# Expert products of 512 columns, on two column groups and into one bank, in a fused attention, mixture and gated-unit kernel

## The chip, the cores and the metric

The kernel runs on one core of a Trainium2 chip. The metric is the device time of one execution in microseconds (us): 532.63 us, the median of three runs (532.57 to 532.8). The trace comes from one more execution, the profiled one.

## What is computed

Three stages follow one another, all in float32.

```python
p_packed = sm_attn(p, k, v)                 # 8 batches, 8 heads, 32 packed queries
x = sm_attn(q, p_packed, p_packed)          # 4608 tokens of 512
logits = x @ phi                            # 32 slots, 4 for each of 8 experts
d = softmax(logits, over tokens)
slot_input = d.T @ x                        # (8, 4, 512)
for e in range(8):
    h = maximum(slot_input[e] @ w1[e], 0)   # w1[e]: 512 x 1024
    slot_out[e] = h @ w2[e]                 # w2[e]: 1024 x 512
x = softmax(logits, over slots) @ slot_out
out = (sigmoid(x @ w_gate) * (x @ w_val)) @ w_out     # d_ff = 1536
```

`sm_attn` is softmax attention. The change lies in the loop over the experts and around it.

## The kernel before

**Stages.** The attention (to about 118 us) works batch by batch after an order written out by hand. The experts follow (to about 161 us), then the gated unit (to the end), which works through units of 768 tokens by 128 columns of `d_ff`, each in three parts. Each part has six products of 512 columns into `o_ps` and one `gate_value` for the unit ahead. Nothing of the gated unit can start before all experts are done: it multiplies by `gst`, which `g_product` makes from the transposed outputs `sot` of all slots.

**Weights.** The weights of the experts lie as 256 blocks of 128 x 256 numbers (128 KB): for each expert 16 blocks of `w1`, then 16 of `w2`. The first 15 blocks come in one transfer into `extra`, the others in 27 transfers `wt` of nine blocks, the last one of seven (blocks 249 to 255). `load` (line 155) gives each transfer a slot of a pool. A slot that is used again has to be read to the end first, and since SyncE issues transfers in the order of the program, one that waits for its slot holds up those behind it. The script's step `loads` issues, after the weights 14 to 25, the three 512 KB pieces of chunk 0 of the gated unit (`wg`, `wv`, `wo`), then the last weights, then the pieces of chunk 1 and of the later chunks. The `wv` of chunk 1 takes the slot that the transfer of blocks 240 to 248 used.

**An expert.** `up(e)` (line 742) has 16 products, for k in 0 to 3 and j in 0 to 3, of 256 columns each. The stationary operand is 32 wide, and j chooses one of four column groups of TensorE, so that the result lies as 4 x 32 partitions by 256 columns. A float32 product is two instructions in the trace. `rectify(e)` (line 756) is ScalarE's ReLU into `hs`. `flip(e)` (line 761) transposes `hs` in two pieces, and VectorE copies the expert's columns into `htz`, which is zero elsewhere. `down(e)` (line 772) has 16 products of 256 columns, for k in 0 to 7 and two halves n, with column group `k % 4`; half n goes into the bank `so_ps[n]`, in which all experts accumulate. In `down(7)`, before block 249, `warm(LAST_WARM)` (lines 663, 777) puts eight filler products of 128 columns.

**Order.** `script` (line 826) gives the order of the steps on every engine; an engine keeps its program order. `up(e)` runs two lines ahead of `down(e - 2)`. Between them lie `cst_turn` (line 713, TensorE transposes the token weights into a bank of `q_g`, of which there are two) and `cst_stack` (line 724, ScalarE and VectorE copy a batch out of it in turns, GpSimd copies on). `turn2` needs the bank that the stacks of batches 0 to 3 read. `decode_open` (line 811) decodes chunk 0: for each of three pieces ScalarE's `high`, VectorE's `shift`, ScalarE's `scale`, VectorE's `add`, and then ScalarE's `w_high` into `wo_parts`. It stands behind `flip7` and before `down7`.

**Tail.** ScalarE and VectorE copy the two halves of `so_ps` into `sos` (lines 869, 870), a short filler follows, then `sot_product` for both halves, copies, `g_product` (16 products on two column groups, 64 wide), another filler, `g_one`, and the gated unit begins. Chunk 1's decode (`a`, `b`, `o`) lies between these on ScalarE and VectorE; `b` is the `wv` of chunk 1.

**Pace.** In the gated unit the generator `readying` (line 931) prepares the weights of later units in small steps, one of which is `g_product`. `pace(part)` (line 1072) says how many steps a part takes, so that each is done when it is due.

Of the kernel before, what the change touches and what calls it, by code (L numbers as in the profile page):

```python
# [35 lines left out]
EPS = 1e-9  # L36
GOES = [(0, 0, 2), (1, 0, 3), (2, 0, 4), (0, 2, 6), (1, 3, 8), (2, 4, NF), (0, 6, NF), (1, 8, NF)]
WARM = 2
LAST_WARM = 8

EXTRA = 15
FIRST_WARM = 4
# [7 lines left out]
def kernel(  # L50
# [101 lines left out]
        places[0] += 1  # L152
        return head if places[0] % (HEADS + RING) in (1, 2) else ring

    def load(dst, key, src, name, last=False):
        i = turn[0] - 3 * B
        turn[0] += 1
        if i < SLOTS:
            r = i % SLOTS
            if r < TWIN:  # L160
                if r == 0:
                    twin.append(keep.tile([128, TWIN * SLOT], F32, name="twin", tag="cst"))
                t = twin[-1][:, SLOT * r : SLOT * r + SLOT]
            else:
                pool = ring if r < TWIN + RING else home if r < TWIN + RING + HOME else more
        elif last:
            pool = next_pool()
        else:

            r = i - SLOTS - HEADS - 3  # L170
            pool = once if r < -1 else spare if r < 0 else ring if r < RING else home if r < RING + HOME else more
            if r < -3:
                pool = head
        if i >= SLOTS or r >= TWIN:
            t = pool.tile([128, WB * EXTRA if pool is spare else SLOT], F32, name=name, tag="w")
        if src.dtype == F32:
            dst[key] = t[:, 0 : src.shape[-1]]
            nc.sync.dma_start(out=dst[key], in_=src)
        else:
# [12 lines left out]
    for i, (x, b) in enumerate("k0 k1 v0 q0 k2 v1 q1 k3 v2 q2 k4 v3 q3 v4 k5 q4 k6 k7 v5 q5 q7 v6 v7 q6".split()):  # L192
        b = int(b)
        for r in (slice(0, 1), slice(1, B))[i : i + 1]:
            nc.sync.dma_start(out=praw[:, r], in_=pd[:, r])
            (nc.gpsimd if i else nc.vector).tensor_scalar_mul(out=praw[:, r], in0=praw[:, r], scalar1=0.125)
        dst, src = dict(k=(kt, kd), v=(vt, vd), q=(qt, qd))[x]
        load(dst, b, src[b], x + "t")
        if i == 1:
            for r in range(2):  # L200
                rows = slice(64 * r, 64 * r + 64)
                nc.sync.dma_start(out=phi[rows, :, r, :], in_=phid[rows])

    def load_weights(a, z):
        for i in range(a, z):
            load(wt, i, wd[:, WB * (EXTRA + WS * i) : WB * min(EXTRA + WS * i + WS, NW)], "wt")

    nc.sync.dma_start(out=extra, in_=wd[:, 0 : WB * EXTRA])
    load_weights(0, SLOTS)
# [412 lines left out]
    q_a = pmid.enter_context(tc.tile_pool(name="q_a", bufs=4, space=PSUM))  # L622
# [36 lines left out]
    def qa():  # L659
        return q_a.tile([128, 512], F32, name="qa", tag="qa")  # L660


    def warm(n=WARM):
        ps = qa()
        for _ in range(n):
            pe.matmul(ps[:, 0:128], lhsT=i16, rhs=i16, start=True, stop=True)

    ps = qa()
    pe.transpose(ps[:, 0:128], prun, ident)
# [59 lines left out]
            for q in (0, 1):  # L729
                pool.tensor_copy(out=s[32 * q + 64 : 32 * q + 96], in_=s[32 * q : 32 * q + 32].bitcast(F32))  # L730

    so_ps = [q_so.tile([128, 512], F32, name=f"so_ps{n}") for n in range(2)]

    def block(e, i):
        i += 32 * e - EXTRA
        if i < 0:
            return extra[:, WB * (i + EXTRA) : WB * (i + EXTRA + 1)]
        return wt[i // WS][:, WB * (i % WS) : WB * (i % WS) + WB]

    hidden = {}  # L740

    def up(e):
        ps = qa()
        for k in range(4):
            for j in range(4):
                pe.matmul(
                    ps[32 * j : 32 * j + 32, 0:WB],
                    lhsT=xt[:, PERM[k], :],
                    rhs=block(e, 4 * k + j),
                    start=k == 0,  # L750
                    stop=k == 3,
                    tile_position=(0, 32 * j),
                )
        hidden[e] = ps

    def rectify(e):
        hs = e2p.tile([128, 256], F32, name="hs")
        act.activation(hs, hidden[e][:, 0:256], AF.Relu, scale=zr)
        hidden[e] = hs

    def flip(e):
        hs, ps = hidden[e], qa()
        for i in range(2):
            pe.transpose(ps[:, 128 * i : 128 * i + 128], hs[:, 128 * i : 128 * i + 128], ident)
        htz = hidden[e] = e2p.tile([128, 4, 2, NS], F32, name="htz")
        dve.memset(htz, 0.0)
        dve.tensor_copy(
            out=htz[:, :, :, 4 * e : 4 * e + 4],
            in_=ps[:, 0:256].rearrange("p (i j s) -> p j i s", i=2, j=4)[:, :, :, 4 * e : 4 * e + 4],
        )  # L770

    def down(e):
        for k in range(8):
            for n in range(2):
                j = k % 4
                if 32 * e + 16 + 2 * k + n == EXTRA + WS * (NWT - 1):
                    warm(LAST_WARM)
                pe.matmul(
                    so_ps[n][32 * j : 32 * j + 32, 0:WB],
                    lhsT=hidden[e][:, k // 2, k % 2, :],  # L780
                    rhs=block(e, 16 + 2 * k + n),
                    start=e == 0 and k < 4,
                    stop=e == E - 1 and k >= 4,
                    tile_position=(0, 32 * j),
                )


    def w_parts(x, f0, n):
# [33 lines left out]
    def split_first():  # L822
# [2 lines left out]

    script = """
        up0 slots_sub sums loads cst_open rectify0 slots_exp
        up1 rectify1 flip0 slots_sum
        up2 rectify2 down0 flip1
        up3 rectify3 down1 flip2 turn0  # L830
        up4 rectify4 down2 flip3 turn1 stack0 stack1
        up5 rectify5 stack2 down3 flip4 stack3
        turn2 up6 rectify6 stack4 down4 flip5 stack5
        down5 flip6 stack6
        up7 rectify7 down6 stack7 flip7 decode_open down7
    """
    steps = dict(up=up, rectify=rectify, flip=flip, down=down, turn=cst_turn, stack=cst_stack)
    alone = dict(
# [27 lines left out]
            )  # L866
        return sot[n].rearrange("p i r s -> p (i r s)"), ps[:, 0:128]

    act.copy(out=sos[0], in_=so_ps[0][:, 0:WB])
    dve.tensor_copy(out=sos[1], in_=so_ps[1][:, 0:WB])  # L870
    w_low(0, 1, w0[2].w)
    a.high()
    a.shift()
    warm()
    s0, s1 = sot_product(0), sot_product(1)
    act.copy(out=s0[0], in_=s0[1])
    dve.tensor_copy(out=s1[0], in_=s1[1])
# [28 lines left out]
    warm()  # L906
    g_one(0, first)
    b.scale()
    a.add()
# [193 lines left out]
    for n, (t, f, a, z) in enumerate(units):  # L1103
# [3 lines left out]
        for part in range(NH):  # L1107
# [95 lines left out]
```

## Time and profile before

| | us |
|---|---|
| median of three runs | 532.63 |
| profiled execution, its own time | 532.35 |
| its span in the trace | 530.6 |
| TensorE busy in the span | 507.0 (96%) |
| VectorE, ScalarE busy | 330.2 (62%), 288.5 (54%) |
| granted TensorE clock, mean | 0.994 of full speed |

The span begins and ends with the program's own instructions; the execution's own time has 1.75 us around it. Times in the rows further down are us from the start of the span. PE is TensorE's products and PEld its weight loads, DVE is VectorE, ACT ScalarE, POOL GpSimd, SP SyncE, which issues transfers. Behind an instruction stands, in brackets, how long its engine had been idle before it and what ended that. The ends of products are modelled, their starts recorded.

### The profile page before, as it was taken

Reading aid. Unit: us, or ns where it says so; the run is one execution under the profiler, and the core shown is the slowest. Engines: PE = TensorE matmul, PEld = TensorE weight load, DVE = VectorE, ACT = ScalarE, POOL = GpSimd, SP = SyncE. Lnnn points to the kernel's source line nnn. Section 1 sums busy time; section 2 is a strip of 40 time slices with the busy share of each in tenths; the row PEclk is TensorE's granted clock in tenths of the full one; section 3 lists DMA queues with packets and bytes.
Section 4 is the critical chain, followed back from the end, with each engine's and each line's share of the span. In section 5 each row is a group of like instructions: output and inputs, shape, how many; then the busy total and the mean of one; then the engine's idle time right before and its main releaser. Section 6 shows DMA issues by size and latency. Waiting matters only on the chain.

```text
span 530.6 us, 10825 instructions
## 1 busy us (share of the span) xinstructions
PE 507.0 (96%) x4217; PEld 394.4 (74%) x4217; DVE 330.2 (62%) x797; ACT 288.5 (54%) x749; POOL 58.4 (11%) x137
## 2 busy tenths in 40 slices
PE   8869989999888999999999999999999999999996
PEld 4536667665546787878888888888888888888885
DVE  2457869864357888889796654674445544454443
ACT  2656777633347878969585444444445444454443
POOL 4021413311540000210101000000000000000000
PEclk9988999999999999999999999999999999999999
DMA  8999999999999163360100120330001200030003
GB/s 326 420 419 418 418 420 419 417 419 418 420 387 397 73 233 119 125 240 13 67 0 1 42 79 1 119 118 3 1 1 41 79 2 0 1 119 2 1 1 119
DMA packets 18642, 91.45 MB, mean 172 GB/s; under 512 B 2336, under 2 KB 2720, under 8 KB 12064
## 3 DMA queue, kind: packets, MB, share of 16 engines
q1 hardware_dynamic: 18592, 90.77, 42.6%
q8 instruction: 33, 0.54, 0.4%
q14 instruction: 17, 0.14, 0.1%
HBM read 81.33 MB, written 9.44 MB: 171 GB/s over the span
## 4 chain that ended last, share of the span: by engine, by line
PE 82%; DMA 10%; DVE 3%; ACT 2%; issue 2%; SPq 0%; DVEq 0%; ACTq 0%
PE o_ps L81 54%; PE qg L81 11%; DMA wt<-in_w_dram 5%; DMA vt<-in_v_dram 3%; PE qa L81 2%; PE pq L81 2%; PE sq L81 2%; PE tq L81 2%; PE tps L81 1%; PE ta L81 1%; PE tp L81 1%; PE lp L81 1%; PE sp L81 1%; DMA kt<-in_k_dram 1%; PE lt L81 1%
## 5 line engine op out<-in xcount | busy, mean ns | idle before, releaser
L81 PE MATMUL o_ps<-wo_parts,gh 128*128 128x512 f32 x864 | 271.5, 395 | 0.5 <-ACT gh L81 0.5
L81 DVE TENSOR_TENSOR gv<-gv,qg 128x256 f32<-128x256 f32 x215 | 89.7, 418 | 126.3 <-ACT gv L81 125.4
L81 PE MATMUL o_ps<-wo_parts,gl 128*128 128x512 f32 x432 | 168.2, 389 | 0.0
L81 ACT ACTIVATE gv<-qg 128x256 f32<-128x256 f32 x215 | 82.5, 385 | 153.3 <-PE qg L81 153.1
L81 PEld LDWEIGHTS o_ps<-wo_parts,gh 128*128 128x128 f32 x864 | 147.8, 189 | 20.4 <-ACT gh L81 0.9
L81 PEld LDWEIGHTS o_ps<-wo_parts,gl 128*128 128x128 f32 x432 | 81.2, 188 | 18.8 <-DVE gl L81 0.3
L81 PEld LDWEIGHTS qg<-cst,gst 128*128 128x128 f32 x430 | 79.4, 188 | 19.5 <-DVE gv L81 1.3
L81 DVE TENSOR_TENSOR gl<-gv,gh 128x256 fp32r<-128x256 f32 (+1 forms) x217 | 90.2, 416 | 0.8 <-ACT gh L81 0.2
L81 ACT CAST gh<-gv 128x256 fp32r<-128x256 f32 (+1 forms) x217 | 86.6, 400 | 4.1 <-DVE gv L81 3.7
L81 PE MATMUL qg<-cst,gst 128*128 128x256 f32 x430 | 86.0, 283 | 0.1
L81 ACT ACTIVATE wgv<-wgv 128x512 f32<-128x512 f32 (+3 forms) x32 | 29.2, 927 | 1.4 <-DMA wgv<-in_wg_dram 1.4
L81 POOL TENSOR_TENSOR a<-ex,sm 128x512 f32<-128x512 f32 (+1 forms) x24 | 21.6, 905 | 25.3 <-DVE sm L81 13.3
L81 POOL CAST gst<-gst 32x128 fp32r<-32x128 f32 x32 | 10.6, 331 | 120.1 <-ACT gst L81 103.6
L81 DVE TENSOR_REDUCE mx<-tq 128x16 f32<-128x512 f32 (+1 forms) x24 | 14.2, 592 | 11.8 <-PE tq L81 11.7
L81 PE MATMUL so_ps<-wt,htz 128*32 128x256 f32 x224 | 14.7, 383 | 2.2 <-DMA wt<-in_w_dram 1.1
L81 DVE TENSOR_REDUCE nmax<-sp 128x1 f32<-128x576 f32 x16 | 11.4, 751 | 8.6 <-PE sp L81 8.6
L81 ACT ACTIVATE head<-sp,nmax 128x576 f32<-128x576 f32 x16 | 11.8, 743 | 8.3 <-DVE nmax L81 8.3
L81 ACT ACTIVATE hs<-qa,zr 128x256 f32<-128x256 f32 x8 | 3.7, 472 | 23.1 <-PE qa L81 16.1
L81 PE MATMUL sq<-qt,ppt 64*32 64x288 f32 x256 | 11.6, 431 | 4.6 <-issue 2.5
L81 ACT ACTIVATE ex<-ex 128x512 f32<-128x512 f32 (+1 forms) x24 | 13.4, 561 | 4.5 <-DVE ex L81 4.3
L81 DVE TENSOR_TENSOR ex<-tq,mx 128x512 f32<-128x512 f32 (+1 forms) x24 | 14.5, 603 | 1.7
L81 DVE TENSOR_REDUCE sm<-ex 128x16 f32<-128x528 f32 (+1 forms) x24 | 14.3, 596 | 1.7 <-ACT ex L81 1.6
(166 smaller groups left out, 519.4 us busy)
## 6 DMA issues: line engine op xcount, KB each, us to landing
wt<-in_w_dram SPq DMA_DIRECT2D x24, 1152.0 KB, 21.9
qt<-in_q_dram SPq DMA_DIRECT2D x8, 1152.0 KB, 22.4
out_dram<-os SPq DMA_DIRECT2D x35, 256.0 KB, 2.1
kt<-in_k_dram SPq DMA_DIRECT2D x7, 1152.0 KB, 18.3
vt<-in_v_dram SPq DMA_DIRECT2D x7, 1152.0 KB, 22.4
wgv<-in_wg_dram SPq DMA_DIRECT2D x5, 1024.0 KB, 7.4
wgv<-in_wv_dram SPq DMA_DIRECT2D x5, 1024.0 KB, 8.6
wo<-in_wo_dram SPq DMA_DIRECT2D x5, 1024.0 KB, 5.0
```

The costliest lines, as they stand in the source:

```text
L81: return lambda *args, **kw: tc.keep_in_program_order(op(*args, **kw))
```

## The change

It has five parts.

1. The second products have 512 columns: `so_ps` is one bank, and `down` has eight products of both halves at once, on the same four column groups. The freed bank goes to `q_a` (5 instead of 4).
2. The first products of experts 2 to 7 have 512 columns and use two column groups: `hs` is 64 x 512, and `flip` has four transposes of 64 x 128. Where two neighbouring blocks lie in two transfers, a product is split into two of 256 columns. `hs` has one buffer instead of two.
3. The last transfer of weights is issued as two, of four and three blocks. The products of the last three blocks, of 256 columns, go to groups of their own. One of the two transfers of `phi` is split as well.
4. The fillers: one product of 512 columns at the head of `down7` instead of eight of 128 columns before block 249; one of 256 columns instead of two of 128 at the two later places.
5. The order of the script, and in the gated unit one step of `readying` that moves from part 6 to part 7.

```diff
-LAST_WARM = 8
+LAST_WARM = 1
+LAST_PIECE = 3
+WIDE = 2
...
         if src.dtype == F32:
-            dst[key] = t[:, 0 : src.shape[-1]]
-            nc.sync.dma_start(out=dst[key], in_=src)
+            n = src.shape[-1]
+            dst[key] = t[:, 0:n]
+            for r in (slice(0, n - cut), slice(n - cut, n))[0 : 1 + (cut > 0)]:
+                nc.sync.dma_start(out=dst[key][:, r], in_=src[:, r])
...
-                rows = slice(64 * r, 64 * r + 64)
-                nc.sync.dma_start(out=phi[rows, :, r, :], in_=phid[rows])
+                for rows in ((slice(0, 64),), (slice(64, 120), slice(120, 128)))[r]:
+                    nc.sync.dma_start(out=phi[rows, :, r, :], in_=phid[rows])
...
+            cut = WB * LAST_PIECE if i == NWT - 1 else 0
...
-    so_ps = [q_so.tile([128, 512], F32, name=f"so_ps{n}") for n in range(2)]
+    so_ps = q_so.tile([128, 512], F32, name="so_ps")
...
     def up(e):
         ps = qa()
+        m = 2 if e >= WIDE else 1
         for k in range(4):
-            for j in range(4):
-                pe.matmul(
-                    ps[32 * j : 32 * j + 32, 0:WB],
-                    lhsT=xt[:, PERM[k], :],
-                    rhs=block(e, 4 * k + j),
-                    start=k == 0,
-                    stop=k == 3,
-                    tile_position=(0, 32 * j),
-                )
+            for j in range(4 // m):
+                parts = blocks(e, 4 * k + m * j, m)
+                for i, x in enumerate(parts):
+                    n = x.shape[-1]
+                    pe.matmul(
+                        ps[32 * j : 32 * j + 32, n * i : n * i + n],
+                        lhsT=xt[:, PERM[k], :],
+                        rhs=x,
+                        start=k == 0 and i == 0,
+                        stop=k == 3 and i == len(parts) - 1,
+                        tile_position=(0, 32 * j),
+                    )
...
     def flip(e):
         hs, ps = hidden[e], qa()
-        for i in range(2):
-            pe.transpose(ps[:, 128 * i : 128 * i + 128], hs[:, 128 * i : 128 * i + 128], ident)
+        n = hs.shape[0]
+        for i in range(256 // n):
+            pe.transpose(ps[:, n * i : n * i + n], hs[:, 128 * i : 128 * i + 128], ident[0:n, 0:n])
...
     def down(e):
+        todo = []
         for k in range(8):
+            i = 32 * e + 16 + 2 * k
+            last = i + 2 > NW - LAST_PIECE
+            parts = [blocks(e, 16 + 2 * k + o, 1)[0] for o in range(2)] if last else blocks(e, 16 + 2 * k, 2)
+            for o, x in enumerate(parts):
+                todo.append((k, i + o, (k + 2 * o * last) % 4, o * x.shape[-1], x))
+        final = {j: n for n, (_, _, j, _, _) in enumerate(todo)}
+        for n, (k, i, j, at, x) in enumerate(todo):
+            if i <= EXTRA + WS * (NWT - 2) < i + x.shape[-1] // WB:
+                warm(LAST_WARM, 4)
+            pe.matmul(
+                so_ps[32 * j : 32 * j + 32, at : at + x.shape[-1]],
+                lhsT=hidden[e][k],
+                rhs=x,
+                start=e == 0 and k < 4 and at == 0,
+                stop=e == E - 1 and final[j] == n,
+                tile_position=(0, 32 * j),
+            )
...
         up0 slots_sub sums loads cst_open rectify0 slots_exp
-        up1 rectify1 flip0 slots_sum
-        up2 rectify2 down0 flip1
-        up3 rectify3 down1 flip2 turn0
-        up4 rectify4 down2 flip3 turn1 stack0 stack1
-        up5 rectify5 stack2 down3 flip4 stack3
-        turn2 up6 rectify6 stack4 down4 flip5 stack5
-        down5 flip6 stack6
-        up7 rectify7 down6 stack7 flip7 decode_open down7
+        up1 flip0 rectify1 slots_sum
+        up2 flip1 rectify2 down0
+        down1 up3 flip2 rectify3 turn0
+        up4 flip3 rectify4 down2 turn1 stack0 stack1
+        up5 flip4 rectify5 stack2 down3 stack3
+        turn2 up6 flip5 rectify6 stack4 down4 stack5
+        flip6 down5 stack6 stack7
+        up7 rectify7 down6 flip7 decode_open down7
...
-    act.copy(out=sos[0], in_=so_ps[0][:, 0:WB])
-    dve.tensor_copy(out=sos[1], in_=so_ps[1][:, 0:WB])
+    act.copy(out=sos[0], in_=so_ps[:, 0:WB])
+    dve.tensor_copy(out=sos[1], in_=so_ps[:, WB : 2 * WB])
...
-    warm()
+    warm(1, 2)
...
                 k = pace(NH * n + part)
+                if NH * n + part == begins[2] - 2 * NH:
+                    k, done[0] = k - 1, done[0] - 1
```

`blocks(e, i, n)` gives n neighbouring blocks as one operand, or as two where they lie in two transfers; `warm(n, m)` gives n fillers of 128 m columns.

## Rows read from the trace of the kernel before

**Rows 1.** The page's 40 slices of 13.3 us: GB/s moved by the transfers

```profile
GB/s 326 420 419 418 418 420 419 417 419 418 420 387 397 73 233 119 125 240 13 67 0 1 42 79 1 119 118 3 1 1 41 79 2 0 1 119 2 1 1 119
```

**Rows 2.** Stretches: length, busy PE, PEld, DVE, ACT, POOL (instructions), PEclk, DMA share, GB/s

```profile
118.90:161.04 42.14, 37.29 (x557) 22.38 (x557) 18.89 (x45) 16.06 (x34) 15.89 (x34) 1.00 1.00 407
...
166.03:530.60 364.57, 359.62 (x1898) 298.56 (x1898) 230.27 (x549) 198.40 (x520) 10.60 (x32) 1.00 0.17 65
```

**Rows 3.** Chain that ended last, 126 to 166 us: start, length, what

```profile
131.05 10.35 DMA wt<-in_w_dram
...
141.46 18.45 DMA wt<-in_w_dram
...
159.95 1.09 PE so_ps L81 x14
```

**Rows 4.** Timeline, TensorE, in the gated unit: start, length, instruction, [idle before]

```profile
180.33 1.09 PE L81 MATMUL qg<-u,sot 128*64 128x128 f32 x14 [0.77 <-DVE u L81]
```

**Rows 5.** Timeline, TensorE, among the experts

```profile
131.26 0.60 PE L81 MATMUL qg<-ident,lall 128*128 128x128 f32 x4
131.79 1.93 PE L81 MATMUL qa<-wt,xt 128*32 128x256 f32 x32
133.54 1.96 PE L81 MATMUL so_ps<-wt,htz 128*32 128x256 f32 x32
...
139.67 0.44 PE L81 MATMUL qa<-ident,hs 128*128 128x128 f32 x2
...
141.54 0.42 PEld L81 LDWEIGHTS qg<-ident,lall 128*128 128x128 f32 x4 [1.68 <-issue]
...
146.68 1.98 PE L81 MATMUL so_ps<-wt,htz 128*32 128x256 f32 x32 [0.47 <-DVE htz L81]
...
148.96 1.06 PE L81 MATMUL qa<-wt,xt 128*32 128x256 f32 x14
151.14 1.27 PE L81 MATMUL qa<-wt,xt 128*32 128x256 f32 x17 [1.12 <-DMA wt<-in_w_dram]
...
154.28 0.44 PE L81 MATMUL qa<-ident,hs 128*128 128x128 f32 x2
...
156.78 2.05 PE L81 MATMUL qa<-i 128*128 128x128 f32 x16
```

**Rows 6.** By tile, `so_ps` and the attention's first filler `wu`: ns least/median/most, starts

```profile
L81 PE MATMUL so_ps<-wt,htz x224: 379/379/405, 129.1 to 160.7; 128*32 128x256 f32 x112
...
L81 PE MATMUL wu<-lall x16: 592/592/1222, 1.4 to 13.6; 128*128 128x512 f32 x16
```

**Rows 7.** Timeline, TensorE, `g_product`

```profile
162.56 1.11 PE L81 MATMUL qg<-w,sot 128*64 128x128 f32 x16
```

**Rows 8.** Timeline, VectorE and ScalarE, decode of chunk 0 and the copy of `so_ps`

```profile
156.01 0.43 DVE L81 TENSOR_SCALAR w<-wgv 128x512 int32<-128x512 int32 x1 [0.70 <-ACT wgv L81]
...
159.02 0.69 DVE L81 CUSTOM_DVE_ANT_0 w<-wo,w 128x1024 uint16<-128x1024 uint16 x1
...
159.74 0.62 ACT L81 CAST wo_parts<-w 128x512 fp32r<-128x512 f32 x1 [0.77 <-DVE w L81]
161.10 0.37 ACT L81 COPY sos<-so_ps 128x256 f32<-128x256 f32 x1 [0.74 <-PE so_ps L81]
...
162.48 0.69 ACT L81 ACTIVATE wgv<-wgv 128x512 f32<-128x512 f32 x1
```

**Rows 9.** Timeline, ScalarE's `rectify5` and VectorE's last read for batches 0 to 3

```profile
138.09 0.47 ACT L81 ACTIVATE hs<-qa,zr 128x256 f32<-128x256 f32 x1 [0.56 <-PE qa L81]
...
140.74 0.84 DVE L81 TENSOR_TENSOR cst<-qg,cst 32x512 fp32r<-32x512 f32 x2
```

**Rows 10.** Timeline, SyncE, `wv` of chunk 1

```profile
156.88 0.33 SPq L183 DMA_DIRECT2D wgv<-in_wv_dram  x1
```

**Rows 11.** Stretches in the attention, columns as in rows 2

```profile
27.00:30.00 3.00, 0.56 (x16) 0.30 (x19) 2.15 (x6) 0.84 (x2) 2.06 (x3) 0.88 0.98 406
30.00:34.00 4.00, 4.00 (x53) 2.13 (x45) 0.40 (x1) 2.02 (x5) 0.60 (x1) 0.66 1.02 424
```

More of the change, by code (lines that the diff above doesn't have):

```diff
@@ L153, in next_pool, with load @@
         return head if places[0] % (HEADS + RING) in (1, 2) else ring
-    def load(dst, key, src, name, last=False):
+    def load(dst, key, src, name, last=False, cut=0):
         i = turn[0] - 3 * B
@@ L200 @@
             for r in range(2):
-                rows = slice(64 * r, 64 * r + 64)
-                nc.sync.dma_start(out=phi[rows, :, r, :], in_=phid[rows])
+                for rows in ((slice(0, 64),), (slice(64, 120), slice(120, 128)))[r]:
+                    nc.sync.dma_start(out=phi[rows, :, r, :], in_=phid[rows])
     def load_weights(a, z):
         for i in range(a, z):
-            load(wt, i, wd[:, WB * (EXTRA + WS * i) : WB * min(EXTRA + WS * i + WS, NW)], "wt")
+            cut = WB * LAST_PIECE if i == NWT - 1 else 0
+            load(wt, i, wd[:, WB * (EXTRA + WS * i) : WB * min(EXTRA + WS * i + WS, NW)], "wt", cut=cut)
     nc.sync.dma_start(out=extra, in_=wd[:, 0 : WB * EXTRA])
@@ L621 @@
     q_so = pmid.enter_context(tc.tile_pool(name="q_so", bufs=1, space=PSUM))
-    q_a = pmid.enter_context(tc.tile_pool(name="q_a", bufs=4, space=PSUM))
+    q_a = pmid.enter_context(tc.tile_pool(name="q_a", bufs=5, space=PSUM))
     gst = low.tile([128, 2, F2], F32R, name="gst")
@@ L660, in qa, with warm @@
         return q_a.tile([128, 512], F32, name="qa", tag="qa")
-    def warm(n=WARM):
+    def warm(n=WARM, m=1):
         ps = qa()
         for _ in range(n):
-            pe.matmul(ps[:, 0:128], lhsT=i16, rhs=i16, start=True, stop=True)
+            rhs = i16[:, None, :].to_broadcast([128, m, 128])
+            pe.matmul(ps[:, 0 : 128 * m], lhsT=i16, rhs=rhs, start=True, stop=True)
     ps = qa()
@@ L730, in cst_stack, with blocks @@
                 pool.tensor_copy(out=s[32 * q + 64 : 32 * q + 96], in_=s[32 * q : 32 * q + 32].bitcast(F32))
-    so_ps = [q_so.tile([128, 512], F32, name=f"so_ps{n}") for n in range(2)]
-    def block(e, i):
+    so_ps = q_so.tile([128, 512], F32, name="so_ps")
+    def blocks(e, i, n):
         i += 32 * e - EXTRA
-        if i < 0:
-            return extra[:, WB * (i + EXTRA) : WB * (i + EXTRA + 1)]
-        return wt[i // WS][:, WB * (i % WS) : WB * (i % WS) + WB]
+        if i + n <= 0:
+            return [extra[:, WB * (i + EXTRA) : WB * (i + EXTRA + n)]]
+        if n == 2 and (i < 0 or i % WS == WS - 1):
+            return [blocks(0, x + EXTRA, 1)[0] for x in (i, i + 1)]
+        return [wt[i // WS][:, WB * (i % WS) : WB * (i % WS + n)]]
     hidden = {}
@@ L754, in up, with hidden_part @@
         hidden[e] = ps
+    def hidden_part(t, e):
+        return t[0:64, :] if e >= WIDE else t[:, 0:256]
     def rectify(e):
-        hs = e2p.tile([128, 256], F32, name="hs")
-        act.activation(hs, hidden[e][:, 0:256], AF.Relu, scale=zr)
-        hidden[e] = hs
+        hs = e2p.tile([128, 512], F32, name="hs", bufs=1)
+        act.activation(hidden_part(hs, e), hidden_part(hidden[e], e), AF.Relu, scale=zr[0:64] if e >= WIDE else zr)
+        hidden[e] = hidden_part(hs, e)
     def flip(e):
@@ L762, in flip @@
         hs, ps = hidden[e], qa()
-        for i in range(2):
-            pe.transpose(ps[:, 128 * i : 128 * i + 128], hs[:, 128 * i : 128 * i + 128], ident)
-        htz = hidden[e] = e2p.tile([128, 4, 2, NS], F32, name="htz")
+        n = hs.shape[0]
+        for i in range(256 // n):
+            pe.transpose(ps[:, n * i : n * i + n], hs[:, 128 * i : 128 * i + 128], ident[0:n, 0:n])
+        htz = e2p.tile([128, 4, 2, NS], F32, name="htz")
         dve.memset(htz, 0.0)
[L767 to L770, printed above, removed]
+        x = ps[:, 0:256].rearrange("p (a b s) -> p a b s", s=NS, b=n // NS)
@@ L772, in down @@
+        if e < WIDE:
+            x = x.rearrange("p i j s -> p j i s")
+        dve.tensor_copy(out=htz[:, :, :, 4 * e : 4 * e + 4], in_=x[:, :, :, 4 * e : 4 * e + 4])
+        hidden[e] = [htz[:, 2 * (k // 2 % 2) + k % 2, k // 4] if e >= WIDE else htz[:, k // 2, k % 2] for k in range(8)]
     def down(e):
+        todo = []
         for k in range(8):
[L774 to L785, printed above, removed]
+            i = 32 * e + 16 + 2 * k
[3 more added lines that the diff above has]
+                todo.append((k, i + o, (k + 2 * o * last) % 4, o * x.shape[-1], x))
@@ L905 @@
     first = g_product(1, (w0[0].w, w0[1].w), [q_g.tile([128, 512], F32, name="qg", tag="qg") for _ in range(2)])
-    warm()
+    warm(1, 2)
     g_one(0, first)
```

## The prediction

> **What bounds the kernel now.** I read the slices first [rows 1]: until about 160 us the DMA engines move some 419 GB/s in nearly every slice, then hardly anything. The stretches [rows 2] give the two halves: DMA share 1.00 from 118.90 to 161.04, and after 166.03 TensorE busy for 359.62 of 364.57 us. The chain of waits [rows 3] runs through TensorE until 131.05, then for 28.8 us through transfers of weights. The last weights land at 159.91 (141.46 + 18.45), their fourteen instructions take 1.09, and five more us pass before the steady products begin. All 364.57 us of the last stage come after the experts, so whatever moves the experts' end moves the kernel's, less the stalls that the last stage has (one of 0.77 us, [rows 4]).
>
> The question is therefore how much room TensorE has beside the transfers between 118.90 and 161.04. It is busy for 37.29 of 42.14 us [rows 2], so 4.85 are idle, and 2.05 of the busy time is the filler of line 777 [rows 5]. That is 6.9 us of room and no more: the stage starts with a backlog, and the first wait of TensorE for weights is at 151.14 [rows 5].
>
> **First products on two groups.** A narrow `up` is 32 instructions of 256 columns over four column groups, eight to a group. Such an instruction lasts 379 ns; one of 512 columns in the same type lasts 592 [rows 6]. So 256 columns more cost 213 ns: 256 columns occupy a group for 213 and 512 for 426, and 379 - 213 leaves 0.17 us of fill. Eight times 213 is 1.71, and an `up` and the `down` behind it start 1.75 apart (131.79 to 133.54 [rows 5]): the four groups really run side by side. Two groups do too: the 16 instructions of 128 columns in `g_product` take 1.11 [rows 7], 59 ns apiece without the fill, about half of the 107 for which one occupies its group. A wide `up` is 16 instructions, eight to a group: 8 x 426 = 3.41, with the same 0.04 on top 3.45. It streams the same columns through half as many groups: 1.70 more, for six experts 10.2 us.
>
> The Trainium skill, TensorE: Matmul & The Clock Gate, section "Part 3: Packing small matmuls — row/col tiling", gives 2.38x for three column tiles, 79% of ideal. The trace disagrees (1.75 us against an ideal 1.71). By that share a wide `up` would be an estimated 4.3 us and the sum some 5 us larger.
>
> **Flips.** Two transposes become four for experts 2 to 7. Four in a row took 0.60, two 0.44 [rows 5]: 0.16 more each, 1.0 in all.
>
> **Second products.** The same columns on the same four groups in half as many instructions: zero by the same arithmetic (1.96 from first start to last end [rows 5], 1.71 of it streaming), 0.1 either way.
>
> **One bank.** ScalarE and VectorE read `so_ps` from two banks. From one they may have to take turns; VectorE's copy would then be ScalarE's 0.37 late [rows 8], while TensorE makes the first `sot_product` from ScalarE's. I take zero; the ends are 0 and 0.4.
>
> **Where TensorE then stands.** Up to the `up` at 131.79 TensorE hardly waits (the chain runs through it until 131.05, [rows 3]), so there every extra us counts in full. From 131.79 to the last flip at 154.28 are 22.49 us [rows 5]. Idle in it: 1.51 before `turn2` (139.67 to 141.54, less 0.36 for a flip), 0.47 at 146.68, and 1.41 for weights (148.96 to 151.14, less 0.77 for 14 instructions). Work is thus 19.1; with 10.2 and the 0.8 of five flips it ends at 161.9. One wait stays. `turn2` needs a bank that `cst_stack` of batches 0 to 3 has read; that ended 3.5 after `rectify5` began (138.09 to 140.74 + 0.84 [rows 9]). `rectify5` moves by four wide `up`s and two flips, 7.1, to 145.2, so the bank is free at 148.7. TensorE is there at 140.1 + 6.8 + 0.5 = 147.4 and waits 1.3: flip 7 starts at 163.2, is done at 163.8, and `htz` is copied near 164.05.
>
> **Last weights in two transfers.** They land at 159.91 as before, since no byte goes from ahead of them; TensorE reaches them after 165. Zero, and so for the four groups of the last three blocks. SyncE gets one issue more here and one for `phi`, each like the 0.33 of [rows 10], both ahead of a queue that needed 18.45 us to land what was put in [rows 3]: zero. Slots come free up to 7 us later, so the last weights may be issued near 148.5 instead of 141.46: the queue still holds bytes for 11 us. Hidden.
>
> **Filler.** Before: 2.05 after nine blocks, in the wait for the last weights. After: one product of 512 columns, two instructions, 0.85, at the head of `down7`, beside the `htz` copy. The two later fillers stream as many columns as before: zero.
>
> **What is late next.** `decode_open` stands in VectorE's order behind the flip's copy. Its six operations ran from 156.01 to 159.71, 3.70 (3.36 by their own durations of 0.43 and 0.69), then ScalarE's 0.62 for `wo_parts`, and behind that on ScalarE the copy of `so_ps` [rows 8]. Before, all this lay inside the wait for the last weights. Now it starts at 164.05; ScalarE's part is done by then, so I take 3.5: 167.55, with the cast 168.2. TensorE begins `down7` at 163.8 + 0.85 = 164.65 and ends it near 166.6. So the copy starts at 168.2 instead of 161.10: 7.1 late. `wv` of chunk 1 waits on SyncE for nine blocks of `down7` (156.88 before [rows 10]), now until 165.7. ScalarE wants it 1.38 after the copy (162.48 less 161.10 [rows 8]), at 169.6. Its 512 KB are 1.25 us at 419 GB/s, which leaves 2.6 for the transfer's start. I take zero; the ends are 0 and 1.
>
> **Pace.** One step of the weights' preparation goes from part 6 to part 7, so that the `g_product` that waited 0.77 for VectorE's `u` [rows 4] comes one part later and its operand is ready. I take -0.8; the other end is +0.5, if the next gate then waits for `gst`.
>
> **Sum.** +7.1 - 0.8 = +6.3 on the profiled execution's 532.35 us is 538.65; the median of the runs is 0.28 above that execution: 538.9.
>
> **Rivals.**
> - *Transfers still set the end* (faster). Everything above hangs on a wide `up` costing 3.45. Of 6.9 us of room 1.0 goes to the flips; if a wide `up` costs less than 1.75 + 5.9/6 = 2.7, TensorE is through before 159.91. The last three blocks, six instructions on four groups, then take 2 x 0.213 + 0.17 = 0.6 instead of 1.09: -0.5, with the pace -1.3, 531.3. For it: the chain through the transfers. Against: 592 ns against 379. Chance 0.13.
> - *The room is exactly used up*: 532.6, within 0.2%. 0.03.
> - *TensorE alone sets the end*, with the decode beside `down7`: 166.6 against 161.04, +5.6, with the pace +4.8: 537.4. For it: only 1.6 separate the two. 0.22.
> - *The clock falls.* It was 0.66 from 30 to 34 us, for part of that at the level of 1.2 GHz, after TensorE had been busy for 0.56 of 3 us [rows 11]; it stayed 1.00 through the idle 1.51 before `turn2` [rows 2, 5]. In the new tail TensorE waits from 166.6 to 168.6 with 0.4 of filler. Lost then: 4 x 0.34 + 3 x 0.12 = 1.7, 540.6. 0.05. The Trainium skill, TensorE: Matmul & The Clock Gate, section "HAM oscillation — how this bites in real kernels", says that idle stretches between bursts bring the lower clock back; the rows show that after the longer gap and not after the shorter.
> - *Slots come free so late that the transfers run dry*, and the last weights land late too: above 541. It needs issues 10 us later than I have them. 0.03.
>
> **How the numbers follow.** The forecast has 0.54. Without the wait for `turn2` (1.3) and the decode (1.6) it would be 536.0, and the smaller terms could take it to 534.8; with the pace gaining nothing and the clock's 1.7 it is 541.4. From 534.8 to 541.4 lie nearly all of the slower cases. 0.2% is 1.1 us, about what a measurement of this kernel can tell from no change. Slower: 0.54 + 0.22 + 0.05 + 0.03 = 0.84; same 0.03; faster 0.13.
>
> **What would show it.** Right: an `up` of experts 2 to 7 of 16 instructions of about 592 ns, 3.5 us long; no wait of TensorE for weights; the last weights landing near 160 and their products some 6 us later; `so_ps` copied near 168 behind `wo_parts`; the stage behind it shorter by 0.8. Wrong: a wide `up` of well under 3 us, or TensorE again waiting for the last weights: then the first rival holds. If the copy follows `down7` directly, it is the third.

## The result, and the profile after

| | before | after |
|---|---|---|
| median of 13 runs each, us | 532.63 | 538.69 |
| lowest to highest, us | 532.38 to 533.46 | 534.52 to 540.79 |
| ratio of the medians, 95% interval | | 1.0103 [1.0078, 1.0128] |
| profiled execution, us (span) | 532.35 (530.6) | 535.78 (533.9) |
| granted TensorE clock, mean | 0.994 | 0.997 |

The kernel is slower by 1.0%, 6.1 us, where 538.9 was predicted. The runs spread over 6.3 us, before over 1.1. The profiled execution lies near the low end of that spread, so its rows are read from the end of the attention on, and the spread is explained further down.

The page after: the group of `up`, and the slices that answer to [rows 1].

```profile
GB/s 325 420 420 418 416 419 420 418 419 418 422 345 296 178 172 127 175 236 2 80 1 1 17 103 0 119 118 2 0 2 30 89 1 1 0 119 1 2 0 119
...
L83 PE MATMUL qa<-wt,xt 128*32 128x512 f32 (+1 forms) x136 | 23.7, 516 | 0.0
```

Stretches of the kernel after, to be held against [rows 2]: the experts, the tail, the gated unit.

```profile
114.50:162.90 48.40, 46.51 (x362) 18.23 (x362) 18.76 (x46) 16.64 (x33) 15.91 (x34) 1.00 0.91 375
162.90:169.46 6.56, 4.65 (x36) 3.23 (x34) 4.21 (x12) 4.74 (x13) 0.00 (x0) 1.00 0.94 348
169.46:533.90 364.44, 359.52 (x1898) 298.43 (x1898) 230.27 (x549) 198.37 (x520) 10.63 (x32) 1.00 0.18 67
```

What sets the pace has changed. Before, transfers were busy all through the experts and TensorE for 37.29 of 42.14 us; now TensorE is busy for 46.51 of 48.40, and the transfers are at 0.91. All that TensorE waited for from 113 us to the end of the kernel after:

```profile
PE qg L83 <- DVE cst L83: 1.7, 1, 1.7
PE qa L83 <- ACT sos L83: 0.7, 1, 0.7
PE o_ps L83 <- DVE gst L83: 0.7, 1, 0.7
PE o_ps L83 <- ACT gh L83: 0.5, 1, 0.5
PE o_ps L83 <- DVE held L83: 0.4, 1, 0.4
PE qa L83 <- DVE xt L83: 0.2, 1, 0.2
```

No weight is in that list. TensorE's timeline after (columns as in [rows 5]) shows the wide `up`s, the wait of `turn2`, and the end of the experts:

```profile
145.38 0.63 PE L83 MATMUL qg<-ident,lall 128*128 128x128 f32 x4 [1.71 <-DVE cst L83]
145.94 3.63 PE L83 MATMUL qa<-wt,xt 128*32 128x512 f32 x18
149.50 0.46 PE L83 MATMUL qa<-ident,hs 64*128 64x64 f32 x4
...
159.14 0.46 PE L83 MATMUL qa<-ident,hs 64*128 64x64 f32 x4
159.53 1.13 PE L83 MATMUL qa<-i 128*128 128x512 f32 x2
160.58 2.37 PE L83 MATMUL so_ps<-wt,htz 128*32 128x512 f32 x22
...
164.32 1.12 PE L83 MATMUL qa<-i,sos 128*128 128x64 f32 x8 [0.74 <-ACT sos L83]
```

From one start to the next a wide `up` takes 3.56 (145.94 to 149.50; 137.78 to 141.34 likewise), a narrow one took 1.75. Behind `flip7` VectorE and ScalarE hold up the copy of `so_ps`, on their timelines after:

```profile
159.74 0.43 DVE L83 TENSOR_SCALAR w<-wgv 128x512 int32<-128x512 int32 x1
...
162.65 0.69 DVE L83 CUSTOM_DVE_ANT_0 w<-wo,w 128x1024 uint16<-128x1024 uint16 x1
164.30 0.42 DVE L83 COPY sos<-so_ps 128x256 f32<-128x256 f32 x1 [0.95 <-ACT sos L83]
```

```profile
163.38 0.62 ACT L83 CAST wo_parts<-w 128x512 fp32r<-128x512 f32 x1 [1.69 <-DVE w L83]
163.90 0.37 ACT L83 COPY sos<-so_ps 128x256 f32<-128x256 f32 x1
...
166.00 1.25 ACT L83 ACTIVATE wgv<-wgv 128x512 f32<-128x512 f32 x2 [0.72 <-DMA wgv<-in_wv_dram]
```

The decode begins when `flip7`'s copy is done, the cast follows it, and only then ScalarE copies `so_ps`, although `down7` ended at 162.95. The last row is `wv` of chunk 1. On the chain after (start, length, what) it is the only transfer behind the attention: ScalarE waited 0.72 us for it.

```profile
162.09 3.89 DMA wgv<-in_wv_dram
166.00 1.25 ACT wgv L83 x2
```

Two more places differ. The 0.77 for `u` [rows 4] is gone, and the next part waits 0.41 for a bank that VectorE holds; and the span ends later behind the last output. Timelines after, TensorE and SyncE, and SyncE before:

```profile
183.28 0.70 PE L83 MATMUL o_ps<-wo_parts,gh 128*128 128x512 f32 x2 [0.41 <-DVE held L83]
...
530.83 0.40 SPq L1123 DMA_DIRECT2D out_dram<-gv  x1
```

```profile
527.85 0.40 SPq L1100 DMA_DIRECT2D out_dram<-gv  x1
```

From that last issue to the end of the span are 3.1 us after (533.9 - 530.83) and 2.7 before (530.6 - 527.85).

**The balance.** The attention ends with VectorE's copy into `xt`, whose start I take as the mark, before and after:

```profile
118.58 0.29 DVE L81 COPY xt<-qa 128x128 f32<-128x128 f32 x1 [0.29 <-PE qa L81]
```

```profile
114.89 0.29 DVE L83 COPY xt<-qa 128x128 f32<-128x128 f32 x1 [0.41 <-PE qa L83]
```

The table holds the traces of all kernels against each other, in us. "Copy" is ScalarE's copy of `so_ps` behind the mark, "tail" from that copy to the first product with `wo_parts` and `gh`, "gated unit" from there to the start of its last product, "close" from that to the end of the span.

| kernel | mark | copy | tail | gated unit | close | time of this execution |
|---|---|---|---|---|---|---|
| before | 118.58 | 42.52 | 4.93 | 360.11 | 4.44 | 532.35 |
| after | 114.89 | 49.02 | 5.56 | 359.66 | 4.79 | 535.78 |
| after_again | 115.61 | 49.01 | 5.54 | 359.64 | 4.80 | 536.47 |
| before_wide | 119.75 | 50.81 | 4.93 | 360.16 | 4.45 | 541.96 |
| wide3 | 114.45 | 45.07 | 6.74 | 359.72 | 4.79 | 532.56 |
| narrow | 117.99 | 44.19 | 7.45 | 359.65 | 4.78 | 535.85 |
| narrow_fill | 115.53 | 45.43 | 5.32 | 359.68 | 4.79 | 532.57 |
| fill_nopace | 119.02 | 41.85 | 5.31 | 360.13 | 4.82 | 532.90 |
| fill_onepiece | 119.18 | 42.03 | 5.04 | 359.63 | 4.52 | 532.20 |
| late_cast | 115.68 | 48.10 | 6.40 | 359.67 | 4.80 | 536.41 |
| light | 116.74 | 39.28 | 6.69 | 360.86 | 4.88 | 530.22 |
| before_pace | 118.57 | 42.86 | 4.93 | 359.63 | 4.44 | 532.20 |

After less before: mark -3.69, copy +6.50, tail +0.63, gated unit -0.45, close +0.35, and 0.1 outside the span: 3.4, which is 535.78 - 532.35. For an attention that ends as in the trace before, the change costs 7.1 us, and the profiled execution would have taken 539.5.

### The profile page after: what moved, and what is told of

Its sections match the earlier page's. It is cut to its first block, busy times and chain, and to the rows that moved or that the text cites. A ratio compares the mean times of both kernels' runs of the same rounds, so it can differ in the third digit from the quotient of the medians.

```text
span 533.9 us, 10423 instructions
## 1 busy us (share of the span) xinstructions
PE 514.1 (96%) x4015; PEld 388.1 (73%) x4015; DVE 330.2 (62%) x797; ACT 289.2 (54%) x749; POOL 58.5 (11%) x137
## 4 chain that ended last, share of the span: by engine, by line
PE 88%; DMA 5%; DVE 3%; ACT 2%; issue 1%; SPq 0%; DVEq 0%; ACTq 0%
PE o_ps L83 55%; PE qg L83 11%; PE qa L83 5%; DMA vt<-in_v_dram 3%; PE so_ps L83 2%; PE pq L83 2%; PE sq L83 2%; PE tq L83 2%; PE tps L83 1%; PE ta L83 1%; PE lp L83 1%; DMA head<-in_p_dram 1%; PE tp L83 1%; PE sp L83 1%; PE lt L83 1%
## 5 line engine op out<-in xcount | busy, mean ns | idle before, releaser
L83 PE MATMUL qa<-wt,xt 128*32 128x512 f32 (+1 forms) x136 | 23.7, 516 | 0.0
L83 ACT ACTIVATE hs<-qa,zr 64x512 f32<-64x512 f32 (+1 forms) x8 | 5.0, 629 | 30.1 <-PE qa L83 23.0
L83 PEld LDWEIGHTS qa<-wt,xt 128*32 128x32 f32 x136 | 7.5, 109 | 12.8 <-issue 10.1
```

Of the source, the lines that this page charges most:

```text
L83: return lambda *args, **kw: tc.keep_in_program_order(op(*args, **kw))
```

## The experiments

The theory: the six wide `up`s alone make the loss, since TensorE has 6.9 us of room and they want 10.8; behind them the decode and then `wv` of chunk 1 set the end. The ratios are against the kernel before, run again beside each kernel. The rivals: the order, the one bank or the late transfers do it. A second question came with the spread: does the end of the experts follow the end of the attention?

**narrow**: all `up`s narrow again, the rest of the change kept.

```diff
-WIDE = 2
+WIDE = 8
```

> The changed kernel with the first products of all experts narrow again (four groups, 256 columns); all else as changed. Theory (a wide up costs 1.70 us more, and six of them use up more than TensorE's room): the expert stage is bound by the transfers again, no wait of a wide up is left, the time falls by 6 to 7 us to about 531.5 (before less 0.5 for the last weights in two transfers and less 0.45 for the stall moved in the gated unit), and the runs lie within 1 us of one another, since the transfers hide where the attention ends. Rival (the rest of the change costs something, the one bank or the order): the time stays at 534 us or more.

Measured: 533.23 (532.41 to 535.85, 10 runs), 1.0019 [1.0005, 1.0033]. Most of the loss is gone, but the level is above what was expected. TensorE's timeline of this kernel, and stretches of it (columns as in [rows 2]):

```profile
159.37 2.77 PE L83 MATMUL so_ps<-wt,htz 128*32 128x256 f32 x12 [3.56 <-DMA wt<-in_w_dram]
```

```profile
150.00:158.50 8.50, 5.82 (x50) 2.12 (x50) 3.00 (x7) 3.52 (x7) 2.92 (x7) 1.00 1.00 394
158.50:168.80 10.30, 9.32 (x43) 5.87 (x44) 4.67 (x11) 4.99 (x12) 0.00 (x0) 0.50 1.00 395
```

TensorE waits for weights again, 3.56 us with no filler in it, and the granted clock falls to 0.50, the level of 1.2 GHz, for the last products and nearly the whole tail (7.45). The rival of the falling clock, which `after` never met (1.00 in its stretches), sits here. The two runs at 535.85 are the two with the lowest mean clock (0.984 and 0.981). The Trainium skill, TensorE: Matmul & The Clock Gate, section "HAM oscillation — how this bites in real kernels", warns of idle stretches between bursts; these rows agree, with 3.56 us idle ahead of the fall.

**before_wide**: the kernel before with the change's `up`, `rectify`, `flip` and `blocks` alone; two banks, fillers, order and transfers as before.

```diff
+WIDE = 2
...
+        m = 2 if e >= WIDE else 1
...
-                    lhsT=hidden[e][:, k // 2, k % 2, :],
+                    lhsT=hidden[e][k],
```

> The kernel before with the first products of experts 2 to 7 on two groups (and the flips and the ReLU that go with them) as its one change; two banks, one last transfer, eight fillers and the old order stay. Theory: this part alone makes the whole loss: 537 to 541 us at the median, the runs spread over several us. Rival (the loss is in the other parts): within 1 us of before, 532 to 533.5.

Measured: 540.9 (537.64 to 542.39, 4 runs), 1.0138 [1.0098, 1.0178]. TensorE's timeline:

```profile
150.69 3.63 PE L82 MATMUL qa<-wt,xt 128*32 128x512 f32 x18
...
167.43 2.05 PE L82 MATMUL qa<-i 128*128 128x128 f32 x16
169.41 1.08 PE L82 MATMUL so_ps<-wt,htz 128*32 128x256 f32 x14
```

The wide `up`s by themselves give the whole loss and, from the mark on, 1.3 us more (541.96 - 119.75 against 535.78 - 114.89): the filler of 2.05 now lies in the path, and the pace is the old one. The order, the one bank and the split transfers are not needed for it.

**wide3**: only experts 5 to 7 wide.

```diff
-WIDE = 2
+WIDE = 5
```

> Experts 5 to 7 wide alone (three instead of six). Theory of TensorE's room: three wide ups and flips cost 5.1 + 0.5 = 5.6 us of the 6.9 us of room less the waits that stay, so the time is near that of six narrow ones, 531.5 to 533.5, and the runs spread more than with none, as attentions that end late are no longer fully hidden. Rival (each wide up costs the kernel 1.7 us whatever the room): 535 to 536.

Measured: 534.97 (532.4 to 537.59, 10 runs), 1.0047 [1.0025, 1.0068]. The median missed the theory's 531.5 to 533.5 and lies at the edge of the rival's 535 to 536. Against a price of 1.7 us for each wide `up` whatever the room speak the two fastest runs (532.4, 532.56), at the level of none wide. The profiled run (532.56) has the earliest attention of all, and even so ScalarE waits in the tail, for both pieces of chunk 1:

```profile
161.54 0.65 ACT L83 ACTIVATE wgv<-wgv 128x512 f32<-128x512 f32 x1 [1.65 <-DMA wgv<-in_wg_dram]
...
162.80 1.24 ACT L83 ACTIVATE wgv<-wgv 128x512 f32<-128x512 f32 x2 [0.46 <-DMA wgv<-in_wv_dram]
```

TensorE waited only 0.74 us for the last weights here: three wide `up`s use the room up. A later attention than this one then goes into the time, which is how I read the spread upwards from 532.4; no trace of a slower run shows it.

**after_again**: the kernel after once more, without an edit, for the spread.

> The changed kernel once more, for a second trace. Theory (the spread of its times comes from where the attention ends, which the transfers of weights hid before): the distance from the end of the attention (the copy into xt) to the first product of the gated unit with gh is again 54.6 us within 0.5, and what the time differs from 535.78 is the difference in the start of xt, 114.89 in the first trace, within 0.5 us. Rival (the spread arises among the experts): the start of xt is the same within 0.5 and the distance differs.

Measured: 536.47. Its attention ended 0.72 later than in the trace of `after`, its time is 0.69 longer, and from the mark to the first steady product it is 54.55 against 54.57. So between these two traces the attention's end goes into the time one to one, and that is how I read the spread of the other runs, of which there is no trace. In the twelve traces of the table the mark lies between 114.45 and 119.75, 5.3 us; before, transfers covered that until 160 us. `narrow_fill` (115.53) and `fill_onepiece` (119.18) do the same work up to the mark and lie 3.65 apart. Whether the change moves the end as well stays open: the three traces of the old program have 118.57 to 119.75, and the split of `phi` was not tried alone.

**narrow_fill**: `narrow` with a filler in the wait for the last weights.

```diff
+            if i <= EXTRA + WS * (NWT - 1) < i + x.shape[-1] // WB:
+                warm(8)
```

> The kernel with all first products narrow, and eight fillers of 128 columns back before block 249, as the kernel before had them (the filler at the head of down7 stays). Theory (with narrow products TensorE waited 3.56 us for the last weights without filler, the granted clock fell to the lower level at 158.5 us, and the copies and products up to the gated unit ran slow): the clock stays at 1.00 from the end of the attention on, sos to the first product with gh is 5.0 to 6.0 us again instead of 7.45, and the time is 532.0 to 532.6 with runs within 1 us. Rival (the tail is late for the chunk's pieces, not for the clock): the distance stays above 6.5 us and the time at 533.

Measured: 532.54 (532.33 to 533.01, 11 runs), 0.9997 [0.9989, 1.0006]. Its stretch from 118 to 161 us has a clock of 1.00, and the spread is as narrow as before's:

```profile
118.00:161.00 43.00, 37.15 (x417) 16.81 (x417) 17.03 (x44) 16.39 (x35) 15.89 (x34) 1.00 1.01 413
```

The last weights' products begin at 159.28 here and at 159.37 in `narrow`, so for the two profiled runs (532.57 and 535.85) the clock makes the difference. That it also makes the 0.69 between the medians is likely from the ranges, but no trace shows it. What is left of the change costs and gains nothing, where 531.3 had been worked out for transfers that still set the end: the tail is 5.32 because chunk 1's pieces land just behind, on ScalarE's timeline:

```profile
161.52 0.70 ACT L83 ACTIVATE wgv<-wgv 128x512 f32<-128x512 f32 x1 [0.19 <-DMA wgv<-in_wg_dram]
...
162.80 1.26 ACT L83 ACTIVATE wgv<-wgv 128x512 f32<-128x512 f32 x2 [0.44 <-DMA wgv<-in_wv_dram]
```

**fill_nopace**: `narrow_fill` without the moved step of the pace.

```diff
-                if NH * n + part == begins[2] - 2 * NH:
-                    k, done[0] = k - 1, done[0] - 1
```

> As narrow_fill, without the step of the preparation that moves from part 6 to part 7. Theory (TensorE's wait of 0.77 for u is bought off by a shorter one of 0.41 for held): 0.4 us slower than narrow_fill, and the wait for u of about 0.8 is back in its trace. Rival (the step changes nothing, or the stage absorbs it): within 0.1 us of narrow_fill.

Measured: 532.96 (532.73 to 533.22, 11 runs), 1.0006 [0.9997, 1.0015]. It is 0.42 above `narrow_fill`, and its gated unit 0.45 longer (360.13 against 359.68). In its list of waits the old one is back:

```profile
PE qg L83 <- DVE u L83: 0.8, 1, 0.8
```

**fill_onepiece**: `narrow_fill` with the last weights in one transfer.

```diff
-LAST_PIECE = 3
+LAST_PIECE = 0
```

> As narrow_fill, with the last weights in one transfer and the last three blocks in the groups of the others. Theory (behind the last weights ScalarE waits for chunk 1's first piece, which lands 1.3 later, so that 0.5 us won before it is lost there): within 0.2 us of narrow_fill, with the copy into sos later by 0.3 to 0.6 and the first product with gh at the same distance from the landing of the last weights within 0.2. Rival (the split shortens the path): 0.5 us slower than narrow_fill.

Measured: 532.26 (532.05 to 534.97, 10 runs), 1.0001 [0.999, 1.0012], 0.28 below `narrow_fill` and so a little outside the 0.2 expected, on the side away from the rival. On the timelines, TensorE's last products of the experts and SyncE's last output:

```profile
160.08 1.07 PE L83 MATMUL so_ps<-wt,htz 128*32 128x256 f32 x8 [1.80 <-DMA wt<-in_w_dram]
...
527.58 0.41 SPq L1125 DMA_DIRECT2D out_dram<-gv  x1
```

In one piece the copy comes 0.25 later (161.21 against 160.96), but the first steady product at 166.24 against 166.28: what the split wins, the wait for chunk 1 takes. And the close is 0.27 shorter (4.52 against 4.79), about the 0.28 between the medians. The split of the last weights gains nothing, and in this pair the close is longer with it.

**late_cast**: the change, with ScalarE's cast into `wo_parts` behind the two copies.

```diff
             x.low()
-        split_first()
...
     dve.tensor_copy(out=sos[1], in_=so_ps[:, WB : 2 * WB])
+    split_first()
```

> The changed kernel with ScalarE's cast of wo_parts behind the copies of so_ps instead of ahead of them. Theory (the decode of chunk 0 holds the copy up by about 1 us, and behind it the landing of wv of chunk 1 sets the end again): the copy into sos starts 47.9 to 48.3 us after xt instead of 49.0, and the first product with gh 54.2 to 54.6 after xt instead of 54.55, since ScalarE still waits for wv. Rival (the decode is what sets the end): the first product with gh is 0.8 to 1.1 earlier too, at 53.5 to 53.8.

Measured: 536.41, one run. ScalarE's timeline:

```profile
163.78 0.37 ACT L83 COPY sos<-so_ps 128x256 f32<-128x256 f32 x1 [1.30 <-PE so_ps L83]
...
166.74 1.22 ACT L83 ACTIVATE wgv<-wgv 128x512 f32<-128x512 f32 x2 [1.23 <-DMA wgv<-in_wv_dram]
```

The copy follows TensorE directly and stands 0.92 nearer to the mark (48.10 against 49.02), so decode and cast did hold it by that much. The first steady product stays where it was, 54.50 behind the mark against 54.57: the wait for `wv` grows from 0.72 to 1.23. So the landing of `wv` sets the end in both kernels, and the decode with its cast ends 0.72 sooner in `after`: taking it away gives nothing. `wv` itself is issued when the ninth block of `down7` has been read, so its landing follows TensorE. What an earlier `wv` would gain was not tried.

**light**: `narrow` with transfers of two blocks in place of nine, all products reading those, and the last weights in one transfer. It shows times only: most of the weights are left out.

```diff
-LAST_PIECE = 3
+LAST_PIECE = 0
...
+            if name == "wt":
+                n, src = 2 * WB, src[:, 0 : 2 * WB]
...
-        return [wt[i // WS][:, WB * (i % WS) : WB * (i % WS + n)]]
+        return [wt[i // WS][:, 0 : WB * n]]
```

> As narrow (all first products on four groups), but each of the 27 transfers of weights brings only its first two blocks (256 KB instead of 1152) and every product reads one of these two; 25 of 33 MB of weights are left out, the work on the engines stays, and the last weights come in one transfer. Theory (the transfers set the end of the kernel before, and TensorE's own work among the experts is some 35 us): no wait for weights, sos 36 to 39 us after xt, the time 525 to 530. On the spread, two theories. First: the attention's end moves from run to run because the engines' instructions are fetched through transfers that are full; with light transfers from about 62 us on it ends earlier than in the traces so far (xt at 114.45 to 119.75), at 113 us or less, and the times lie within 2 us of one another. Second: it moves for reasons of its own, such as the granted clock; then xt stays within 114 to 120 and the times spread by 4 us or more.

Measured: 530.22 in the profiled run (529.63 to 531.44 in the three compared; a fourth took 537.87, with the lowest mean clock of the four, 0.981), 0.9956 [0.994, 0.9973]. Copy (39.28) and time lie just above what was expected. TensorE's longest waits from 113 us on, none for weights, and its `down7`:

```profile
PE qg L83 <- DVE cst L83: 1.5, 1, 1.5
PE qa L83 <- ACT sos L83: 1.5, 1, 1.5
PE o_ps L83 <- DVE gst L83: 1.2, 1, 1.2
```

```profile
152.39 1.95 PE L83 MATMUL so_ps<-wt,htz 128*32 128x512 f32 x18
```

Without waits for transfers narrow experts end 37.6 behind the mark (154.34 less 116.74), those of the change 48.06: 10.5 apart, where six wide `up`s at 1.81 more would be 10.9. On the spread the first theory's 113 us or less fell: the attention ended at 116.74. Three of the times lie within its 2 us of one another, the fourth does not. But in this trace the load is light only from about 78 us on (416 GB/s from 66 to 78, 68 from 90 to 102), behind the place where the traces differ (57 to 76 us, further down). Whether full transfers move the attention's end is therefore not settled.

The clock fell here too: it is 0.50 from 158.5 to 165 us. A filler that takes 0.70 at 154.27 takes 1.22 there:

```profile
158.72 1.22 PE L83 MATMUL qa<-i 128*128 128x256 f32 x2
```

So part of the long tail (6.69) and of the 1.2 us more in the gated unit (360.86) go with the clock; the experts' end at 154.34 lies ahead of the fall.

**before_pace**: the kernel before with the moved step of the pace alone.

```diff
+                if NH * n + part == begins[2] - 2 * NH:
+                    k, done[0] = k - 1, done[0] - 1
```

> The kernel before with the step of the preparation moved from part 6 to part 7 as its one change. Theory: it keeps the transfers' hiding of the attention and gains the 0.4 us of the stall: 532.2, faster than both kernels, its stage from the first product with gh on 359.7 instead of 360.1 long. Rival (the gain depends on the other parts): 532.6.

Measured: 532.2 (531.95 to 532.64, 11 runs) against 532.56, 0.9992 [0.9983, 1.0001]. The gated unit, in a stretch (before: 364.57 [rows 2]):

```profile
166.36:530.40 364.04, 359.48 (x1898) 298.39 (x1898) 230.26 (x549) 198.37 (x520) 10.61 (x32) 1.00 0.18 65
```

This has the lowest median of those that leave nothing out, 6.5 us below the change. Of the 0.4 below the kernel before the interval does not rule out zero; the stage, 0.48 shorter in the traces, speaks for it. `fill_onepiece`, which adds the one bank, the wide second products, the fillers and the order to it, has 532.26: no gain from those parts can be told here.

## Why the prediction was right

Counted from the mark, its steps and the rows after, in us:

| step | predicted | measured |
|---|---|---|
| a wide `up`, start to start | 3.45 | 3.56 |
| four small transposes against two | +0.16 | +0.02 |
| wait of `turn2` | 1.3 | 1.71 |
| `flip7` starts | 44.6 | 44.25 |
| decode can start | 45.5 | 44.85 |
| `down7` ends | 48.0 | 48.06 |
| copy of `so_ps`, against before | +7.1 | +6.50 |
| tail, against before | 0 (0 to 1) | +0.63 |
| gated unit, against before | -0.8 (to +0.5) | -0.45 |
| one issue more each for the last weights and `phi` | 0 | +0.35 in the close |

- **Wide `up`: right.** Eight instructions of 426 ns to a group make 3.41 of the 3.56, so the two groups run side by side, and the two that lie idle make them no faster. The range that the rival of a cheap wide `up` needed (under 2.7) is far off. The Trainium skill, TensorE: Matmul & The Clock Gate, section "Part 3: Packing small matmuls — row/col tiling", gives 2.38x for three column tiles, 79% of ideal; by that share a wide `up` would be an estimated 4.3, and the trace disagrees with its 3.56.
- **Flips: too dear.** The four transposes of 64 x 128 take 0.46, two of 128 x 128 took 0.44. The rows that were used were four of the larger kind.
- **Room: right. The decode behind it: right for the copy, not for the end.** No wait for weights is left, and the copy stands behind `wo_parts`, 0.95 after `down7` ended. It came 0.6 sooner than predicted: `flip7` started 0.4 earlier and was 0.14 shorter. The first steady product did not follow it; `wv` held that up.
- **One bank: zero, as taken.** VectorE has been idle for 0.95 when its copy starts, 0.40 after ScalarE's, which has just ended; before, from two banks, it started 0.04 after (161.14 against 161.10). TensorE's eight products behind it take 1.12 against 1.10 in `before_wide`'s two banks, so nobody pays. The Trainium skill, PSUM — Partial Sum Buffer, section "PSUM bank collisions raise a hardware error", says that the compiler back end's scheduler adds a dependency between instructions of two engines on the same bank and quadrant (32 partitions), two reads included; the order in these rows agrees.
- **`wv` of chunk 1: taken as zero, 0.63 in the tail.** From issue to landing it took 3.89, where 1.25 and 2.6 of start had been allowed, 3.85. But ScalarE wanted it 0.72 sooner than it landed, because the copy ahead of it came 0.6 sooner and the issue did not. This is within the ends that were given. The prediction had both paths meet 51.0 behind the mark (169.6 - 118.58); `wv` landed at 51.1 (165.98 - 114.89), and the decode's path was ready 0.72 sooner. So it is this term, put at zero, that set the end, and `late_cast` shows it.
- **Pace: half.** The wait of 0.77 went, 0.41 for `held` came in its place. Both `fill_nopace` (0.42) and `before_pace` (0.36) give the net. The prediction named `gst` as the next to be late; it was the bank.
- **One issue more on SyncE: "zero" left out the end of the program.** From the last output's issue to the end of the span it is 0.35 longer in `after`, and 0.27 of that goes with `fill_onepiece`. The number of transfers alone does not explain it: `light` has its last weights in one transfer too, and a close of 4.88.

The sum for the profiled execution was +6.3; with equal attention it is +7.1. Copy (-0.6) and tail (+0.6) cancel because `wv` set the end where the decode had been expected to; the pace (+0.35), the close and the rest (+0.45) make the 0.8 between the sums. That the median came out within 0.2 all the same is luck and has a cause that **the prediction never named**: it took the attention's end from one trace, 118.58, where the transfers hid it, and that end varies. From 539.5 for 118.58, the median of 538.69 stands for an end near 117.8. The range of 534.8 to 541.4 was made from the terms' bounds; single runs covered 534.52 to 540.79 for another reason.

The rivals: "transfers still set the end" has its conditions in `narrow_fill`, and its price was 1.2 too low (above all chunk 1's pieces 0.4, the pace 0.35 and the close 0.35). "TensorE alone" fails by `wv`: even where the copy follows `down7` directly (`late_cast`), the first steady product comes 54.50 behind the mark, 7.05 later than before (47.45), where that rival had 5.6. The clock fell in `narrow` and `light`, not in `after`; the price of 1.7 that the prediction gave it stands on two terms (0.34 and 0.12) without rows, and in `narrow` it was 3.3.

## What to carry to other kernels

In this kernel a packed product cost its columns over the groups that streamed at once: half the groups at twice the width took twice the time (3.56 us against 1.75), and half as many instructions did not pay for that. Before work is put on an engine beside a transfer-bound stage, count its idle time there, including the backlog it starts with, and remember that the transfers hid not only that engine's work but also the variation of what came before. What lies behind the hidden engine (here a decode, a cast and a late transfer) enters the path with it, and only the one that ends last counts: taking the cast away moved the copy by 0.92 and the end by 0.07.

## What was not expected of the hardware

- **The attention's end differs by up to 5.3 us between the traces**, and by 3.65 where the work ahead of it is the same. The traces differ in TensorE's idle stretches between 57 and 76 us. A stretch from 40 to 76 us of before and after:

```profile
40.00:76.00 36.00, 32.81 (x643) 23.02 (x640) 27.89 (x65) 24.56 (x64) 8.56 (x13) 0.96 1.01 419
```

```profile
40.00:76.00 36.00, 35.80 (x685) 24.27 (x683) 30.12 (x72) 27.40 (x72) 10.62 (x17) 0.96 1.02 419
```

  TensorE is busy for 3.0 us more in `after`, at the same clock (0.96) and the same load of transfers (419 GB/s), which is most of the 3.69 by which its attention ended sooner. Two of the idle stretches, on TensorE's timeline before:

```profile
66.69 0.38 PE L81 MATMUL tp<-ident,head 128*128 128x128 f32 x2 [1.05 <-issue]
...
74.72 1.21 PE L81 MATMUL sq<-qt,ppt 64*32 64x288 f32 x32 [2.14 <-ACT head L81]
```

  The first waited for nothing that the profile shows. The second waited for ScalarE. Why an execution has them or not stays open; `light`, with a mark of 116.74, has two of them as well (1.06 and 1.85, both for nothing that the profile shows).
- **A split of the last weights went with an end of the program 0.3 us longer** (the close: 4.79 in `narrow_fill` against 4.52 in `fill_onepiece`). `light`, without the split, has 4.88, so the cause stays open.
- **With 3.56 us of idle TensorE the clock fell for ten us** (`narrow`), and with a filler of 2 us in the same place it did not (`narrow_fill`): 3.3 us between their profiled runs. In `light` it fell 2 us after an idle of 1.47, while in `after` it stayed at 1.00 through one of 1.71.
